# Decode attention over two key-value caches: the V loads move to ScalarE's DMA queue

## The chip, the cores and the metric

The kernel runs on one core of one Trainium2 chip. The metric is the device time of one execution in microseconds. The core has five engines with an instruction stream each (TensorE, or PE; VectorE, or DVE; ScalarE, or ACT; GpSimd, or POOL; SyncE, or SP) and 16 DMA engines that move data between HBM and the core's SBUF. A DMA is issued by an instruction in the stream of SP or ACT[...].

## The reference

Two problems, A and B, each one decode step of attention with 32 heads, a head size of 128 and one query. The caches have 16,384 keys. A attends to all of them, B to the last 4,096.

```python
q = (x @ wq).reshape(B, Sq, Hq, Dh)            # transposed to heads first
scores = jnp.einsum("bhqd,bhkd->bhqk", q, k) * (Dh ** -0.5)
p = _softmax(scores, axis=-1)
o = jnp.einsum("bhqk,bhkd->bhqd", p, v)
return o.reshape(B, Sq, Hq * Dh) @ wo          # transposed back first
```

In B, k and v are `cache[:, :, Sk - W:, :]` with W = 4096. All of it is bf16: K and V of A are 134 MB each, of B 34 MB each, wq and wo 4 MB for each problem. The two outputs of 512 numbers are joined.

## The kernel before

The caches are read in 20 loads, 16 for A and 4 for B, numbered i = 0 to 19; each has a K part and a V part of 8.39 MB. A load of A is two heads: a partition holds 256 keys of 128 numbers in one run of 64 KB, and 64 partitions hold a head. A load of B is two DMAs (U = 2, u = 0 and 1) of four heads each, with runs of 32 KB. Three buffers of 64 KB per partition take them: `kt` has two slots, K(i) going to slot (i+1) mod 2, and `vt` is one buffer for V. Before V(0), `vt` holds wq; after V(18) it takes wo. The last V, V(19), goes to the slot of `kt` that K(18) has left. `_alloc` lays this out.

Each engine runs a program written out by hand, and semaphores order them. The work on load i:

- VectorE multiplies K(i) by the query in place (`mult`, L304, 17.2 us in A; two instructions of 8.7 us in B), then adds the two halves of the head size in place (`add`, L315). Between the two it reduces the previous load's result to scores (`scores(i-1)`, L321), and after them it collects the previous load's output (`pick(i-1)`, L335 to L342). So its order is mult(i), scores(i-1), add(i), pick(i-1). Loads 0 and 1 are cut into four and two parts.
- TensorE sums the remaining 64 products in PSUM (`red(i)`, 32 matmuls), then multiplies the probabilities by V (`pv(i)`, 64 matmuls), then adds the picked result to `f`. Its order is red(i), pv(i), pick's matmul, red(i+1). After load 15 and after load 19 it normalises a problem (`norm`), and last come the products with wo, first of A, then of B in five pieces. Nearly all its matmuls are recorded under one helper's line, L379.
- ScalarE computes the exps of load i once scores(i) is there (L233): two for an A load, eight for a B load. It also copies the queries out of PSUM (L222), scales the output rows (`_orow`, L248) and issues the loads of x (L216).
- GpSimd only makes constants and passes on counts between VectorE and TensorE.
- SyncE issues all other DMAs, in `_sync_program`. It waits in order: K(i) goes out when red(i-2) has freed its slot (semaphore `s_red`); V(i-1) goes out next, when pv(i-2) has freed `vt` (`s_pv`). K(1) and V(0) wait for the end of the matmuls that read wq (`s_q`). V(19) goes out when red(18) is done. Then SP waits for pv(18) and issues the seven pieces of wo, and last the output.

All loads by SP go through one DMA queue, so the data of K(1), V(0), K(2), V(1) and so on arrive in this order.

In the lists above "pv(i)" means both halves u for a B load. The semaphores of V are `s_v[u]`, and `s_vlast[u]` for V(19); TensorE waits for them before the matmuls of pv.

Of the kernel before, what the change touches and what calls it, by code (L numbers as in the profile page):

```python
# [20 lines left out]
NB = 4  # L21
# [98 lines left out]
def _slot(i):  # L120
    return (i + 1) % 2


def _p_view(cx, st, u):
    return cx.p[u][:, 0 : st.keys * st.R].rearrange("p (t g e) -> p t g e", g=st.R, e=4)


def _sync_program(nc, cx, loads):
    e = nc.sync
    stA, stB = cx.sts  # L130
    for st in cx.sts:
        st.s_wq.on(e.dma_start(out=st.wq_t, in_=st.wq.rearrange("(p c) f -> p c f", c=st.KC)), 16)

    def kv(st, i, which):
        j = i if st is stA else i - stA.L
        view = st.k_view if which == "k" else st.v_view
        last = which == "v" and i == len(loads) - 1
        for u in range(st.U):
            h0 = (j * st.U + u) * st.R
            k0 = u * st.keys  # L140
            if which == "k":
                out = cx.kt[:, _slot(i), k0 : k0 + st.keys, :]
                sem = cx.s_k[_slot(i)][u]
            elif last:
                out = cx.kt[:, _slot(i - 1), k0 : k0 + st.keys, :]
                sem = cx.s_vlast[u]
            else:
                out = cx.vt[:, k0 : k0 + st.keys, :]
                sem = cx.s_v[u]
            ins = e.dma_start(out=out, in_=view[h0 : h0 + st.R].rearrange("g (i l) d -> i g l d", l=st.keys))  # L150
            sem.on(ins, 16)

    pv = 0
    kv(loads[0], 0, "k")
    for i in range(1, len(loads)):
        if i == 1:
            cx.s_q.wait(e, stA.N // stA.R // 512 + stB.N // stB.R // 512)
        else:
            cx.s_red.wait(e, NB * (i - 1))
        kv(loads[i], i, "k")  # L160
        if i > 1:
            pv += loads[i - 2].U
            cx.s_pv.wait(e, pv)
        kv(loads[i - 1], i - 1, "v")
    n = len(loads)
    cx.s_red.wait(e, NB * (n - 1))
    kv(loads[-1], n - 1, "v")
    cx.s_pv.wait(e, pv + loads[-2].U)
    for st, j0, m, sem in cx.pieces:
        src = st.wo.rearrange("(p j) f -> p j f", j=st.J)  # L170
        sem.on(e.dma_start(out=st.wo_t[:, j0 : j0 + m, :], in_=src[:, j0 : j0 + m, :]), 16)  # L171
    for st in cx.sts:
        st.s_row.wait(e, len(st.out_at))
        cx.s_end.on(e.dma_start(out=cx.out[0, 0:1, st.at : st.at + st.DN], in_=cx.row[0:1, st.at : st.at + st.DN]), 16)
    cx.s_end.wait(e, 32)
# [35 lines left out]
def _scalar_program(nc, cx, loads):  # L211
    e = nc.scalar
    stA, stB = cx.sts
    cx.s_pool.wait(e, 1)
    for w, st in enumerate(cx.sts):
        st.s_x.on(e.dma_start(out=cx.row[0:1, w * st.D : (w + 1) * st.D], in_=st.x[0, 0:1, :]), 16)  # L216
    n = 0
    for st in cx.sts:
        m = st.N // st.R // 512
        n += m  # L220
        cx.s_q.wait(e, n)
        st.s_qall.on(e.copy(st.qall[:, :], cx.red[:, 0:m, :].rearrange("p j f -> p (j f)")))  # L222
    cx.s_dve.wait(e, cx.n_off)
    for i, st in enumerate(loads):
        if i == stA.L:
            _orow(e, cx, stA)
        cx.s_sc.wait(e, i + 1)
        j = i if st is stA else i - stA.L
        for u in range(st.U):
            p = _p_view(cx, st, u)  # L230
            for g in range(st.R):
                h = st.f_at + (j * st.U + u) * st.R + g
                ins = e.activation(  # L233
                    out=p[:, :, g, :],
                    in_=cx.sc[:, u * st.keys : (u + 1) * st.keys].rearrange("p (t e) -> p t e", e=4),
                    func=ACT.Exp, scale=SCALE, bias=st.off[:, g : g + 1], accum_out=cx.cs[:, h : h + 1],
                )
            cx.s_p.on(ins)
    _orow(e, cx, stB)
    w = stB.DN // 2  # L240
    stB.s_o.wait(e, 1)
    stB.s_row.on(e.copy(cx.row[0:1, stB.at + w : stB.at + 2 * w], cx.out_ps(stB)[1]))


def _orow(e, cx, st):
    at = st.f_at
    st.s_recip.wait(e, 1)
    st.s_orow.on(e.activation(  # L248
        out=cx.orow[at : at + H, :], in_=cx.f[at : at + H, 0:DH], func=ACT.Copy, scale=cx.recip[at : at + H, 0:1],
    ))  # L250
# [233 lines left out]
def kernel(  # L484
# [49 lines left out]
    cx.out_ps = lambda st: [cx.red[r : r + 1, b, 0 : st.DN // len(st.out_at)] for r, b in st.out_at]  # L534

    _sync_program(nc, cx, loads)
    _pool_program(nc, cx)
    _vector_program(nc, cx, loads)
    _scalar_program(nc, cx, loads)
    _tensor_program(nc, cx, loads)  # L540

# [29 lines left out]
```

The softmax here doesn't subtract the row's maximum and nothing guards it: scores larger than these inputs give would overflow.

## Time and profile before

| what | value |
|---|---|
| time, median of 3 runs (range) | 822.37 us (822.32 to 822.43) |
| the profiled execution: time, and its span from first to last instruction | 822.22 us, 820.0 us |
| busy: PE, DVE, ACT, POOL | 341.2, 603.8, 35.5, 4.3 us |
| read from HBM | 352.32 MB, 430 GB/s over the span |
| mult of A, each (x, with the parts) | 13,810 ns mean of 20; a whole one 17.23 us |
| waits of DVE's mult for K of A | 150.7 us in 15 waits |
| waits of SP's K and V issues for pv, for red | 423.4 us in 18, 304.1 us in 20 |
| from issue to landing, median: K of A, V of A | 37.2 us, 31.3 us |

The profile gives one execution. Its rows name an engine, a line of the kernel, the operation, the output and the inputs by the program's names; "SPq" and "ACTq" are rows of an instruction queue that issues a DMA. A row of the timeline begins with its start and its length in us, and ends, in brackets, with the idle time of the engine before it and what ended that. A landing time counts from the issue, so it includes whatever stands ahead in the queue. The waits of SP are long because it has nothing else to do.

### The profile page before, as it was taken

Reading aid. Unit: us, or ns where it says so; the run is one execution under the profiler, and the core shown is the slowest. Engines: PE = TensorE matmul, PEld = TensorE weight load, DVE = VectorE, ACT = ScalarE, POOL = GpSimd, SP = SyncE. Lnnn points to the kernel's source line nnn. Section 1 sums busy time; section 2 is a strip of 40 time slices with the busy share of each in tenths; the row PEclk is TensorE's granted clock in tenths of the full one; section 3 lists DMA queues with packets and bytes.
Section 4 is the critical chain, followed back from the end, with each engine's and each line's share of the span. In section 5 each row is a group of like instructions: output and inputs, shape, how many; then the busy total and the mean of one; then the engine's idle time right before and its main releaser. Section 6 shows DMA issues by size and latency. Waiting matters only on the chain. (4 is left out here: it accounts for less than half of the span.)

```text
span 820.0 us, 5953 instructions
## 1 busy us (share of the span) xinstructions
PE 341.2 (42%) x2149; PEld 128.6 (16%) x2149; DVE 603.8 (74%) x167; ACT 35.5 (4%) x134; POOL 4.3 (1%) x14
## 2 busy tenths in 40 slices
PE   3433346152424244352608071534243353616276
PEld 1110112020101011110202020211011121202022
DVE  2089995959595968768595959595959969696921
ACT  0100000000000000000000000000000001010110
POOL 2000000000000000000000000000000000000000
PEclk9855668595856675656766575958566766756589
DMA  9999999999999999999999999999999999999997
GB/s 384 436 457 412 457 412 457 412 454 416 454 416 451 416 451 419 451 419 448 422 441 429 435 435 428 441 419 451 416 454 411 456 412 435 435 435 435 435 423 325
DMA packets 8222, 352.41 MB, mean 430 GB/s; under 512 B 916, under 2 KB 920, under 8 KB 1304
## 3 DMA queue, kind: packets, MB, share of 16 engines
q1 hardware_dynamic: 8212, 352.33, 99.4%
q8 instruction: 4, 0.07, 0.0%
q14 instruction: 2, 0.02, 0.0%
q10 hardware_dynamic: 4, 0.00, 0.0%
HBM read 352.32 MB, written 0.00 MB: 430 GB/s over the span
## 5 line engine op out<-in xcount | busy, mean ns | idle before, releaser
L304 DVE TENSOR_TENSOR kt<-kt,qallA 128x32768 bf16<-128x32768 bf16 (+2 forms) x20 | 276.2, 13810 | 150.7 <-DMA kt<-in_A_k_cache_dram 150.7
L379 PE MATMUL acc<-vt,p 128*8 128x512 bf16 (+1 forms) x1216 | 113.1, 550 | 348.3 <-PEq L42 348.3
L379 PE MATMUL red<-kt,ident 128*128 x640 | 183.2, 457 | 43.1 <-PEq L42 43.1
L315 DVE TENSOR_TENSOR kt<-kt 128x16384 bf16<-128x16384 bf16 (+2 forms) x24 | 174.5, 7269 | 0.8
L379 PEld LDWEIGHTS acc<-vt,p 128*8 128x8 bf16 (+1 forms) x1216 | 37.1, 114 | 423.5 <-issue 416.5
L379 PEld LDWEIGHTS red<-kt,ident 128*128 128x128 bf16 x640 | 72.5, 113 | 150.3 <-issue 103.6
L304 DVE TENSOR_TENSOR kt<-kt,qallB 128x16384 bf16<-128x16384 bf16 x8 | 69.5, 8691 | 13.4 <-DMA kt<-in_B_k_cache_dram 13.4
L321 DVE TENSOR_REDUCE sc<-red 128x256 f32<-128x2048 f32 x20 | 45.7, 2284 | 8.0 <-PE red L379 8.0
L233 ACT ACTIVATE p<-sc,offA 128x256 bf16<-128x256 f32 x32 | 16.0, 500 | 604.5 <-DVE sc L321 604.5
L379 PE MATMUL f<-s,win 128*32 128x128 f32 x48 | 11.2, 323 | 62.4 <-PEq L42 62.4
L379 PE MATMUL red<-vt,kt 128*128 128x512 bf16 x64 | 16.1, 416 | 4.6 <-DMA vt<-in_A_wq_dram 2.5
L233 ACT ACTIVATE p<-sc,offB 128x128 bf16<-128x128 f32 x32 | 12.4, 389 | 113.4 <-DVE sc L321 113.4
L342 DVE TENSOR_REDUCE s<-acc 128x128 f32<-128x512 f32 x24 | 16.6, 691 | 0.8
L379 PEld LDWEIGHTS f<-s,win 128*32 128x32 f32 x48 | 4.2, 121 | 72.9 <-issue 72.6
L337 DVE TENSOR_TENSOR acc<-acc,maskA 128x512 f32<-128x512 f32 x16 | 11.1, 692 | 0.0
L335 DVE COPY win<-selB 128x32 f32<-128x32 f32 x8 | 1.4, 178 | 11.3 <-PE acc L379 11.3
L379 PEld LDWEIGHTS red<-vt,kt 128*128 128x128 bf16 x64 | 6.6, 105 | 13.7 <-issue 7.8
L379 PE MATMUL red<-vt,ocA 128*1 128x512 bf16 x32 | 7.2, 379 | 0.0
L379 PE MATMUL acc<-kt,p 128*16 128x512 bf16 x64 | 5.3, 505 | 4.3 <-PEq L42 4.3
L335 DVE COPY win<-selA 128x32 f32<-128x32 f32 x16 | 2.8, 174 | 5.4 <-PE acc L379 5.4
L233 ACT ACTIVATION_READ_ACCUMULATOR p<-sc,offB 128x1 f32 x32 | 6.0, 187 | 0.0
L233 ACT ACTIVATION_READ_ACCUMULATOR p<-sc,offA 128x1 f32 x32 | 6.0, 187 | 0.0
(47 smaller groups left out, 36.8 us busy)
## 6 DMA issues: line engine op xcount, KB each, us to landing
kt<-in_B_k_cache_dram SPq DMA_DIRECT2D x8, 4096.0 KB, 34.8
vt<-in_B_v_cache_dram SPq DMA_DIRECT2D x6, 4096.0 KB, 29.0
kt<-in_B_v_cache_dram SPq DMA_DIRECT2D x2, 4096.0 KB, 36.6
vt<-in_A_wq_dram SPq DMA_DIRECT2D x1, 4096.0 KB, 12.2
vt<-in_B_wq_dram SPq DMA_DIRECT2D x1, 4096.0 KB, 21.4
vt<-in_A_wo_dram SPq DMA_DIRECT2D x2, 2048.0 KB, 23.1
vt<-in_B_wo_dram SPq DMA_DIRECT2D x1, 2048.0 KB, 29.7
vt<-in_B_wo_dram SPq DMA_DIRECT2D x1, 1024.0 KB, 31.6
```

The lines of the kernel that those rows point to most:

```text
L233: ins = e.activation(out=p[:, :, g, :], in_=cx.sc[:, u * st.keys : (u + 1) * st.keys].rearrange("p (t e) -> p t e", e=4), func=ACT.Exp, sc ...
L304: n = did(e.tensor_tensor(out=k, in0=k, in1=q.rearrange("p (o d) -> p o d", o=1).broadcast_to([P, b - a, DH]), op=ALU.mult,))
L315: cx.s_half.on(e.tensor_tensor(out=k[:, :, 0 : DH // 2], in0=k[:, :, 0 : DH // 2], in1=k[:, :, DH // 2 : DH], op=ALU.add,))
L321: cx.s_sc.on(e.tensor_reduce(out=cx.sc[:, :], in_=cx.red[:, :, :].rearrange("p b (k w) -> p (b k) w", w=W), axis=AX.X, op=ALU.add,))
L335: did(e.tensor_copy(cx.win[u][:, :], st.sel[:, at : at + H]))
L337: n = did(e.tensor_tensor(out=acc, in0=acc, in1=st.mask[:, :].rearrange("p (x o) -> p x o", o=1).broadcast_to([P, 4, DH]), op=ALU.mult,))
L342: cx.s_pick.on(e.tensor_reduce(out=cx.s[u][:, :], in_=acc.rearrange("p x d -> p d x"), axis=AX.X, op=ALU.add,))
L379: mm = lambda *a, **k: e.matmul(*a, skip_group_check=True, **k)
```

## The change

The function that issues a K or V part becomes `_kv`, which takes the issuing engine as an argument. SP keeps wq, all K parts, wo and the outputs. The V parts are issued in ScalarE's program, before the exps of the same load: V(0) after the copies of the queries, V(i) after a wait for pv(i-1), V(19) after a wait for red(18). The waits are the same as SP's were. ScalarE's issues go to its own DMA queue. Buffers, sizes and the programs of the other engines stay as they are.

```diff
-    pv = 0
-    kv(loads[0], 0, "k")
+    _kv(e, cx, loads, 0, "k")
     for i in range(1, len(loads)):
         if i == 1:
             cx.s_q.wait(e, stA.N // stA.R // 512 + stB.N // stB.R // 512)
         else:
             cx.s_red.wait(e, NB * (i - 1))
-        kv(loads[i], i, "k")
-        if i > 1:
-            pv += loads[i - 2].U
-            cx.s_pv.wait(e, pv)
-        kv(loads[i - 1], i - 1, "v")
-    n = len(loads)
-    cx.s_red.wait(e, NB * (n - 1))
-    kv(loads[-1], n - 1, "v")
-    cx.s_pv.wait(e, pv + loads[-2].U)
+        _kv(e, cx, loads, i, "k")
+    cx.s_pv.wait(e, sum(st.U for st in loads[:-1]))
     for st, j0, m, sem in cx.pieces:
...
     for i, st in enumerate(loads):
         if i == stA.L:
             _orow(e, cx, stA)
+        if i == len(loads) - 1:
+            cx.s_red.wait(e, NB * i)
+        elif i:
+            cx.s_pv.wait(e, sum(s.U for s in loads[:i]))
+        _kv(e, cx, loads, i, "v")
         cx.s_sc.wait(e, i + 1)
```

`_kv` has the body of the nested `kv`, with `e` as the issuing engine and the load's index in place of its problem:

```python
def _kv(e, cx, loads, i, which):
    st = loads[i]
...
    for u in range(st.U):
...
        ins = e.dma_start(out=out, in_=view[h0 : h0 + st.R].rearrange("g (i l) d -> i g l d", l=st.keys))
        sem.on(ins, 16)
```

More of the change, by code (lines that the diff above doesn't have):

```diff
@@ L125, in _p_view @@
     return cx.p[u][:, 0 : st.keys * st.R].rearrange("p (t g e) -> p t g e", g=st.R, e=4)
+def _kv(e, cx, loads, i, which):
+    st = loads[i]
+    stA = cx.sts[0]
+    j = i if st is stA else i - stA.L
+    view = st.k_view if which == "k" else st.v_view
+    last = which == "v" and i == len(loads) - 1
+    for u in range(st.U):
+        h0 = (j * st.U + u) * st.R
+        k0 = u * st.keys
+        if which == "k":
+            out = cx.kt[:, _slot(i), k0 : k0 + st.keys, :]
+            sem = cx.s_k[_slot(i)][u]
+        elif last:
+            out = cx.kt[:, _slot(i - 1), k0 : k0 + st.keys, :]
+            sem = cx.s_vlast[u]
+        else:
+            out = cx.vt[:, k0 : k0 + st.keys, :]
+            sem = cx.s_v[u]
+        ins = e.dma_start(out=out, in_=view[h0 : h0 + st.R].rearrange("g (i l) d -> i g l d", l=st.keys))
+        sem.on(ins, 16)
 def _sync_program(nc, cx, loads):
@@ L132, in _sync_program @@
         st.s_wq.on(e.dma_start(out=st.wq_t, in_=st.wq.rearrange("(p c) f -> p c f", c=st.KC)), 16)
[L134 to L151, printed above, removed]
-    pv = 0
-    kv(loads[0], 0, "k")
+    _kv(e, cx, loads, 0, "k")
     for i in range(1, len(loads)):
```

## The prediction

> **What bounds the kernel now.** I read the page first: its slices, its queue table and its chain.
>
> ```profile
> DMA  9999999999999999999999999999999999999997
> ...
> q1 hardware_dynamic: 8212, 352.33, 99.4%
> ...
> DMA vt<-in_B_wo_dram 4%; PE acc L379 0%; SPq L171 0%; DVE row L373 0%; PE red L379 0%
> ```
>
> The 16 DMA engines are full in every slice but the last, all on one queue (q1, SP's), and the chain ends in the wo load. Two stretches of the trace give the rate (columns: stretch, length, busy time of PE, PEld, DVE, ACT, POOL, clock, DMA share, GB/s):
>
> ```profile
> 330.00:640.00 310.00, 125.87 (x792) 46.70 (x790) 242.70 (x49) 8.74 (x32) 0.00 (x0) 0.67 1.00 433
> 640.00:780.00 140.00, 58.13 (x376) 21.73 (x378) 115.28 (x36) 11.02 (x53) 0.00 (x0) 0.67 1.00 434
> ```
>
> So 434 GB/s whatever the engines do. A load of K or V (128 rows x 65,536 B = 8.39 MB) takes 19.3 us, a K and V pair 38.6 us; 352.3 MB take 812 of the 820.0 us. No order of the same bytes saves more than the few us at the ends. What an order can do is leave DMA with nothing to do. For that I read when SP issues, and what VectorE does:
>
> ```profile
> 1.90 30.12 SPq L150 DMA_DIRECT2D kt<-in_A_k_cache_dram  x2
> 32.07 0.61 SPq L150 DMA_DIRECT2D vt<-in_A_v_cache_dram  x1
> 73.67 0.54 SPq L150 DMA_DIRECT2D kt<-in_A_k_cache_dram  x1
> 87.79 0.54 SPq L150 DMA_DIRECT2D vt<-in_A_v_cache_dram  x1
> 110.86 0.54 SPq L150 DMA_DIRECT2D kt<-in_A_k_cache_dram  x1
> ```
>
> ```profile
> 371.92 17.23 DVE L304 TENSOR_TENSOR kt<-kt,qallA 128x32768 bf16<-128x32768 bf16 x1 [9.10 <-DMA kt<-in_A_k_cache_dram]
> ...
> 410.51 17.23 DVE L304 TENSOR_TENSOR kt<-kt,qallA 128x32768 bf16<-128x32768 bf16 x1 [9.02 <-DMA kt<-in_A_k_cache_dram]
> ```
>
> K(9) lands at 371.9 (mult starts), K(10) at 410.5. After K(9), pv(8) ends and V(9) is issued at 398.13 (+26.2); red(9) ends and K(11) is issued at 411.63 (+39.7). In one queue the order is K(10), V(9), K(11): at 398.13 K(10) still needs 12.4 us, at 411.63 V(9) needs 18. That is the cover; VectorE idles 9 us per cycle. It is the late issue of a load, not work, that could hurt.
>
> [...] the trace shows 434, so I expect no gain in rate. The trace shows the turns once, at the start:
>
> ```profile
> 1.92 0.51 ACTq L216 DMA_DIRECT2D row<-in_A_x_dram  x1
> ...
> 8.01 0.29 PE L379 MATMUL oc_ps<-one,row 1*128 1x1 bf16 x4 [2.45 <-DMA row<-in_A_x_dram]
> ```
>
> A 1 KB load on ACT's queue, issued at 1.92 behind 8.4 MB of wq and 8.4 MB of K(0), is there at 8.01, when even the first wq (13.2, by its 12.2 us to landing) is not. So ACT's queue goes between SP's, though some packets late: 6.1 us for 1 KB is what some four wq packets of 1.2 us take (32 KB each; estimate from 434 GB/s over 16 engines). K and V packets of problem A are equal (64 KB), so the shares are half and half.
>
> **The change part by part.**
>
> *Removed from SP, added on ACT.* Twenty-four V issues (0.54 us per A load, 1.18 per B pair, from SP's rows) move to ScalarE, which is busy 35.5 of 820 us. They run before the wait for scores: nothing. V(i)'s wait for pv(i-1) adds nothing for the exps behind it: scores(i) comes after pick(i-1) on VectorE, which waits for pv(i-1) anyway. V(16) now stands behind orow of A: 667.5 becomes 670.3, 2.8 us, under other loads: nothing, at most 3. K no longer stands behind V's waits on SP, but K's wait (red) is met before V's (pv), so K's issue rule is unchanged.
>
> *Moved in time: the sharing.* V no longer stands behind the K issued before it but takes half the engines. No bytes more; but K lands later, and what K's landing releases is issued later.
>
> *Start.* V(0) is issued at 32.6, once ScalarE's copies end (31.50 + 1.01). K(0) (lands 43.7), K(1) and V(0) are 50 us of data from 31.5, done at about 81 in any order. In one queue K(1) was there by 63, before VectorE could take it (70.3). In turns K(1) lands last, at 82: mult(1) is 11.7 us late, so V(1)'s issue goes from 87.8 to 99.5 and K(3)'s from 110.9 to 122.5. DMA then has K(2) alone (issued at 73.7): 81 to 100.3; V(1), about 1 us after its issue, 100.6 to 119.9; K(3) at 123.6. Nothing moves for 0.3 + 3.7 us. If V(0) cuts into K(0) too, K(0) lands at 50 and V(0) at 74, K(1) still at 82; red(0) and so K(2) come 7 us later, still within 81. I take 4.5 us; bounds 3 and 6.
>
> *Middle.* I stepped the loads forward with offsets from before: K(i) lands, exps(i-1) end 20.6 later; pv(i-1), 5.9, starts when they and V(i-1) are there and issues V(i); red(i) ends 40 after K(i)'s landing and issues K(i+2); first data 1 after an issue; half rate while both queues have work. One pair of cycles: K(5) lands at 222, exps(4) end at 242.6, V(4) lands at 243.5, pv(4) issues V(5) at 249.4. K(6) has been alone from 243 and lands at 263; red(5) issues K(7) at 262, which shares with V(5). V(5) lands at 289.5, pv(5) issues V(6) at 295.4, and K(7) lands at 299; then the pattern repeats. K's intervals alternate between 41 and 36, mean 38.6. The tightest point is the last: K(7)'s data end at about 298, V(6)'s begin at 296.4, so some 2 us of cover are left of 12. As long as it holds the middle costs nothing.
>
> *End.* V(19) took the slot of K(18) and was issued at 755.61 by SP. On ACT it stands behind the exps of load 18:
>
> ```profile
> 755.61 1.18 SPq L150 DMA_DIRECT2D kt<-in_B_v_cache_dram  x2
> 781.37 0.81 SPq L171 DMA_DIRECT2D vt<-in_A_wo_dram  x2
> ```
>
> Those end at 772.7 in the trace, 17 us after 755.61. The same stepping brings V(17) at 756, by its sharing and the start's 4.5 us, so pv(17) ends at 759 (before 743); then pick 1.5, mult(19) 17.3 (before it waited for K(19) until 748.9), scores 2.3, exps 3.3: V(19) is issued at about 784. K(19) and V(18) are done at 782.5 (before 778, plus 4.5); V(19)'s data start at 785 to 786: 3.5 us dry (bounds 0 and 5). wo is issued after pv(18), at 789; with wo rows of 16 KB and V rows of 32 KB, V(19) has two thirds of the engines from some 790 on: 4.3 us of its 19.3 are done, the other 15 take 22, so it lands near 812. wo ends when both are through, 786 + 38.6 + 1 = 826.
>
> PE then becomes the end. Before:
>
> ```profile
> 803.46 7.24 PE L379 MATMUL red<-vt,ocA 128*1 128x512 bf16 x32
> 812.01 1.91 PE L379 MATMUL red<-vt,ocB 128*1 128x256 bf16 x32 [1.31 <-DMA vt<-in_B_wo_dram]
> ...
> 816.90 0.38 PE L379 MATMUL red<-vt,ocB 128*1 128x256 bf16 x4 [0.21 <-DMA vt<-in_B_wo_dram]
> ```
>
> PE's products with wo come after pv(19) in program order, 7.24 + 1.91 + 1.04 + 1.03 + 0.38 = 11.6 us, and waited for wo. Now: V(19) at 812, last half of pv 2.7, picks and norm 3.0 (800.5 to 803.5 before): 817.7; products to 829.3; copy and store 2.7 (817.3 to 820.0 before): 832. By wo alone it would be 826 + 0.4 + 2.7 = 829.
>
> *Sum.* Dry 4.5 + 3.5, products past the last wo 3: 11; the chain of the end by itself gives 832 - 820 = 12. I take 11.5, a span of 831.5. The profiled execution took 822.22 with its span of 820.0; 822.22 + 11.5 = 833.7. The runs' median is 822.37, 0.15 more, below the rounding of the steps.
>
> **Rivals.**
>
> *Not slower.* The engines take whole transfers in order of issue. Then K(1) precedes V(0) as now, nothing is dry, and V(19), 17 us later, still comes before V(18) ends at 778 and before wo: 822.4. It decides if K(1) lands before 70.3. Against it: the 1 KB load above.
>
> *The middle dries out.* The margin of 2 us is gone, because shares are unequal or an issue takes longer to start. One us lost per cycle on some 15 cycles gives 833.7 + 15 = 849. At the extreme, V always first, the same steps lose 9.7 us on every second cycle: 895. For it: the margin is thin. Against: equal packets.
>
> *The rate falls.* Two streams of 64 KB rows on one engine cost 1%: 812 x 0.01 = 8 us more, 842. Nothing in the trace shows it; the rate was 433 and 434 in the two stretches, with rows of 64 and 32 KB.
>
> *Faster.* Only a rate over 434[...]. Then the losses above must be absent as well.
>
> **How the numbers follow.** Forecast 0.70 (its own range 828 to 838), not slower 0.09, middle dry 0.11, rate 0.08, faster 0.02. About 0.2% (1.6 us) is what a measurement of this kernel can tell from no change. Slower by more: 0.70 + 0.11 + 0.08 = 0.89; within: 0.09; faster: 0.02. The range 827 to 843 takes in the forecast with the bounds of its costs (dry 3 to 11, products 0 to 3) and the rate case; it leaves out the not-slower case and the dried-out middle.
>
> **What would show it.** ACT's queue with some 168 MB (20 loads of 8.39); mult(1) at about 82 with a wait for K; K(3) issued near 122; intervals of K that alternate but average 38.6; 434 GB/s in the middle; V(19) issued near 784; the chain ending in PE's wo products, not in DMA. Wrong: K(1) landing at 63, a middle average over 39, or a rate off 434.

## The result and the profile after

The changed kernel took 843.48 us at the median of four runs (840.08 to 847.53), beside 822.35 for the kernel before: a ratio of 1.0259, interval 1.0212 to 1.0306, slower. A second series of five runs gave 842.27 (840.37 to 845.07), ratio 1.0245 (1.0225 to 1.0264). So the loss is some 20 us where 11.5 were forecast, and its direction is the forecast's. The runs of the changed kernel lie up to 7 us apart; those of the kernel before lie within 0.2 us. The profiled execution is the slowest of the first four (847.53, span 845.3), so what is read from it is somewhat more than the median loses.

On its page the queue table now has two rows, and the chain (by engine) no longer begins with DMA:

```profile
q1 hardware_dynamic: 4756, 184.55, 50.8%
q10 hardware_dynamic: 3460, 167.78, 46.7%
...
PE 2%; DVE 0%; ACT 0%; issue 0%
```

q10 is ScalarE's queue, with the 167.8 MB of V. The two shares add to 97.5% of the span, 99.4% before. Where the rest went is read from two stretches, the start and the loads 2 to 15. Before, then after (columns as above: the last two are DMA share and GB/s):

```profile
14.00:130.00 116.00, 48.92 (x257) 17.90 (x255) 84.69 (x21) 5.06 (x10) 0.00 (x0) 0.69 1.00 434
130.00:640.00 510.00, 205.71 (x1293) 76.64 (x1294) 391.26 (x81) 14.21 (x52) 0.00 (x0) 0.67 1.00 434
```

```profile
14.00:130.00 116.00, 44.95 (x194) 16.43 (x192) 73.76 (x18) 3.97 (x6) 0.00 (x0) 0.64 0.95 407
130.00:640.00 510.00, 186.30 (x1274) 70.14 (x1274) 385.92 (x79) 14.20 (x52) 0.00 (x0) 0.70 1.00 427
```

At 434 GB/s the first stretch would have needed 116 x 407 / 434 = 108.8 us: 7.2 are lost at the start. The second loses 510 x (1 - 427 / 434) = 8.2, where the prediction had nothing. The remaining 10 us are after 640. Note that the DMA share still reads 1.00 in the second stretch: the rows that DMA moves took longer there, which is taken up below.

VectorE's waits show what became late (longest in total, times, longest one):

```profile
DVE win L335 <- PE acc L379: 113.2, 18, 11.8
DVE kt L304 <- DMA kt<-in_A_k_cache_dram: 87.4, 14, 39.0
```

Before, VectorE waited 150.7 us for K of A and 16.8 us for pv (the row `win` is the first instruction of pick). Now the larger wait is for pv, which waits for V. The half-and-half share is seen when queue shares are taken from a stretch in which K and V are both under way, 53 to 68 us (columns: rows, which the page calls packets and which are 64 KB here, MB, and their time as a share of the 16 engines'):

```profile
q10 hardware_dynamic: 51, 3.34, 51.4%
q1 hardware_dynamic: 49, 3.21, 49.4%
```

The start went as follows:

```profile
51.46 4.43 DVE L304 TENSOR_TENSOR kt<-kt,qallA 128x8192 bf16<-128x8192 bf16 x1 [39.04 <-DMA kt<-in_A_k_cache_dram]
...
82.73 8.69 DVE L304 TENSOR_TENSOR kt<-kt,qallA 128x16384 bf16<-128x16384 bf16 x1 [4.54 <-DMA kt<-in_A_k_cache_dram]
```

K(0) is taken at 51.5 (43.7 before), K(1) at 82.7 (70.3 before). And the end: the last two V issues and, from the chain in order of time, PE's products with wo.

```profile
791.10 0.54 ACTq L146 DMA_DIRECT2D kt<-in_B_v_cache_dram  x1
...
791.67 0.62 ACTq L146 DMA_DIRECT2D kt<-in_B_v_cache_dram  x1
```

```profile
830.30 12.33 PE red L379 x92
```

V(19) is issued at 791.1; the last products begin when pv(19) is through, and take 12.3 us to the end's copy and store.

### The profile page after: what moved, and what is told of

Read it like the earlier page. It is cut to its first block, busy times and chain, and to the rows that moved or that the text cites. A ratio compares the mean times of both kernels' runs of the same rounds, so it can differ in the third digit from the quotient of the medians.

```text
span 845.3 us, 5952 instructions
## 1 busy us (share of the span) xinstructions
PE 328.6 (39%) x2149; PEld 124.6 (15%) x2149; DVE 604.3 (71%) x167; ACT 35.5 (4%) x134; POOL 4.3 (1%) x14
## 5 line engine op out<-in xcount | busy, mean ns | idle before, releaser
L379 PE MATMUL acc<-vt,p 128*8 128x512 bf16 (+1 forms) x1216 | 110.7, 541 | 389.1 <-PEq L42 389.1
L379 PE MATMUL red<-kt,ident 128*128 x640 | 171.2, 427 | 51.1 <-PEq L42 51.1
L379 PEld LDWEIGHTS red<-kt,ident 128*128 128x128 bf16 x640 | 68.2, 107 | 149.8 <-issue 101.1
L233 ACT ACTIVATE p<-sc,offB 128x128 bf16<-128x128 f32 x32 | 12.4, 388 | 113.1 <-DVE sc L321 113.1
L379 PE MATMUL acc<-kt,p 128*16 128x512 bf16 x64 | 7.2, 627 | 9.0 <-PEq L42 9.0
L379 PE MATMUL red<-vt,ocA 128*1 128x512 bf16 x32 | 9.7, 479 | 0.0
```

What stands on the lines that cost most here:

```text
L233: ins = e.activation(out=p[:, :, g, :], in_=cx.sc[:, u * st.keys : (u + 1) * st.keys].rearrange("p (t e) -> p t e", e=4), func=ACT.Exp, sc ...
L379: mm = lambda *a, **k: e.matmul(*a, skip_group_check=True, **k)
```

## The experiments

Each run stands beside runs of the kernel before on the same chip.

| run | what it does | us, median | over before | ratio (interval) |
|---|---|---|---|---|
| v0_sp | V(0) back on SP's queue | 840.59 | 18.3 | 1.0232 (1.0212 to 1.0252) |
| vlast_sp | V(19) back on SP's queue | 847.41 | 25.1 | 1.0304 (1.0282 to 1.0325) |
| both_sp | V(0) and V(19) back | 843.36 | 21.1 | 1.0255 (1.0231 to 1.0279) |
| both_sp_pvhalf | the same, pv of A halved | 836.03 | 13.8 | 1.0172 (1.0153 to 1.0191) |
| before_vlate | one queue, V(19) issued late | 822.19 | 0.0 | 1.0000 (0.9991 to 1.0008) |
| before_pv2 | one queue, pv of A twice | 822.14 | -0.1 | 1.0000 (0.9992 to 1.0009) |
| after_pv2 | changed kernel, pv of A twice | 861.04 | 38.8 | 1.0474 (1.0458 to 1.0490) |
| mid_only | only V(1) to V(15) on ACT's queue | 833.90 | 11.7 | 1.0153 (1.0134 to 1.0171) |
| mid_only_pvhalf | the same, pv of A halved | 829.12 | 6.9 | 1.0087 (1.0073 to 1.0101) |
| mid_only_k32 | mid_only, K rows of 32 KB | 861.99 | 39.8 | 1.0484 (1.0466 to 1.0502) |
| mid_only_v32 | mid_only, V rows of 32 KB | 894.96 | 72.7 | 1.0886 (1.0871 to 1.0901) |
| after_again | the changed kernel again | 842.27 | 20.0 | 1.0245 (1.0225 to 1.0264) |
| end_sp | V(16) to V(19) back on SP's queue | 836.99 | 14.7 | 1.0182 (1.0165 to 1.0199) |
| v8_only | only V(8) on ACT's queue | 824.06 | 1.8 | 1.0023 (1.0012 to 1.0034) |

### Single loads put back

In `_sync_program`, after the K issue, and with the load taken out of ScalarE's loop:

```diff
         _kv(e, cx, loads, i, "k")
+        if i == 1:
+            _kv(e, cx, loads, 0, "v")
+    cx.s_red.wait(e, NB * (len(loads) - 1))
+    _kv(e, cx, loads, len(loads) - 1, "v")
     cx.s_pv.wait(e, sum(st.U for st in loads[:-1]))
```

(v0_sp has the first two new lines, vlast_sp the last two, both_sp all four.)

> V(0) alone goes back to SP's queue, behind K(1); the other V loads stay on ACT's. Theory 'empty queues' (what the change costs is time in which neither queue has work, because sharing delays what releases the next issues: about 6.6 us at the start, about 8 in the middle, the rest from V(19) on): K(0) lands at 43 and K(1) before 70 again, the dry stretch at 80 to 84 and at 123 goes, and the time falls by about 6, to 837 (835 to 839). Rival 'slower packets' (two queues make the engines themselves slower, whatever the order): 842 to 844.

> V(19) alone goes back to SP's queue, ahead of wo, issued when red(18) is done. 'Empty queues': V(19) no longer waits for the exps of load 18 and no longer shares with wo, so PE's products with wo again wait for wo and not for V(19): 8 us less, 836 (834 to 839). 'Slower packets': within 2 us of the changed kernel, 842.

> V(0) and V(19) both on SP's queue; only V(1) to V(18) are on ACT's. 'Empty queues': the middle's share stays, where V(i) lands late, pv follows at once and V(i+1) is issued when K's data have just ended: 8 us over the kernel before, 830 (827 to 832), and less even from run to run than the kernel before. The prediction's own step (the middle costs nothing): 823. 'Slower packets': 838 or more.

v0_sp missed both ranges: 840.6. The stretch from 14 to 130 us is back at 434 GB/s, but the time falls by 2 to 3 us, not by 6. A little of the gain is lost again later: from 130 to 640 us this run has 426 GB/s, where the changed kernel's profile has 427, which is 1.2 us of the 510.

vlast_sp missed, in the other direction: 847.4. SP's queue is now busy with V(19) while ACT's queue has V(18), and V(18) lands later; that it has half the engines, as V(0) had from 53 to 68 us (51 and 49 rows), is an estimate: its share was not read here. PE's pv(18) shows the delay (the row is its second half):

```profile
805.88 3.53 PE L380 MATMUL acc<-vt,p 128*16 128x512 bf16 x32 [9.97 <-PEq L42]
```

In the changed kernel both halves were done at 797.0; here V(18)'s second half is taken only at 805.9. All that follows pv(18) is a chain of its own: in the kernel before, pv(18) ends at 781.3 and the program at 820.0. It was covered by wo's data there; now V(18)'s lateness goes straight into it. both_sp missed as well: 843.4, where 830 was expected and 823 by the prediction's step. That is a number which 'slower packets' had allowed (838 or more); the time of a row, below, speaks against it.

### What costs in one queue

```diff
     cx.s_red.wait(e, NB * (n - 1))
+    cx.s_sc.wait(e, n - 1)
     kv(loads[-1], n - 1, "v")
```

> The kernel before, with one wait more: SP issues V(19) only when scores(18) are there, some 14 us later than before, about as late as ScalarE's order makes it, but still in the one queue. 'Sharing' (late issues cost nothing while the queue holds V(18), and only the sharing of the engines between two queues costs): 822.3, within 0.5. 'Late issue' (the order of ScalarE's program costs by itself): 826 to 830.

822.2, with V(19) issued at 769.6 instead of 755.6. A V(19) that is 14 us late costs nothing by itself: in one queue V(18) still lies ahead of it (in the kernel before PE takes V(18)'s second half at 778.1). So the wait for the exps, which ScalarE's order puts before V(19), is not the loss at the end as long as there is one queue.

The second pair doubles pv:

```diff
-            for t in range(T):
+            for t in [*range(T)] * (2 if st is stA else 1):
```

> The kernel before, with the product with V of problem A made twice over (128 matmuls instead of 64, the second pass starting anew, so the output is the same): pv takes some 11.5 us instead of 5.7. One queue: V(i) is issued when K(i+1) still has 12.4 us to go, K when V has 18, so 6 us more are covered: 822.3 to 823. If pv were on the path in one queue too: 16 x 5.7 = 91 us more.

> The changed kernel, with the product with V of problem A made twice over as in the run beside it. 'pv in the loop' (with two queues V(i) lands late, pv follows at once, and V(i+1) can be issued only then, so that every us of pv is a us without work for DMA): 4 to 5 us more per load of A, 880 to 920. The prediction's cover of 2 us plus what the sharing gives back: 850 to 865. pv not in the loop: 842 to 848.

With the longer pv the kernel before keeps 822.1, the changed one goes from 842 to 861. pv took 8.8 us instead of about 5.7 (not 11.5 as expected), so 3.1 us more per load cost 19 us over 16 loads, 1.2 us each. 861 lies in the range given for the prediction's cover, but that range was worked out for 5.8 us more per load. What is shown is that pv stands in the loop, and that not every us of it is lost. The stretch from 130 to 640 us, before_pv2 and then after_pv2:

```profile
130.00:640.00 510.00, 229.13 (x2149) 89.79 (x2141) 391.42 (x82) 14.22 (x52) 0.00 (x0) 0.76 1.00 434
```

```profile
130.00:640.00 510.00, 213.36 (x2082) 83.69 (x2082) 368.63 (x78) 14.21 (x52) 0.00 (x0) 0.75 0.96 408
```

The first has more PE work in the same time than the second and a full DMA; the second has 408 GB/s.

### The middle by itself

mid_only issues V(1) to V(15) from ScalarE and all other V from SP, in the order of the kernel before:

```diff
         _kv(e, cx, loads, i, "k")
+        if i == 1 or i > stA.L:
+            if i > 1:
+                cx.s_pv.wait(e, sum(st.U for st in loads[: i - 1]))
+            _kv(e, cx, loads, i - 1, "v")
+    cx.s_red.wait(e, NB * (len(loads) - 1))
+    _kv(e, cx, loads, len(loads) - 1, "v")
```

> Only V(1) to V(15) on ACT's queue; V(0) and V(16) to V(19) back in SP's, in the order of the kernel before. Start and end are then as before, with the last data some 3 us ahead of the end: 822.4 plus the middle's loss, which the account of the profiles puts at 7 to 8: 829 to 832. If the middle costs nothing by itself, 823. If the loss simply moves (as in the runs with V(0) or V(19) alone on SP's queue), 838 or more.

833.9, somewhat above the 829 to 832 expected, and the end is again that of the kernel before, a chain through wo's DMA. Its middle has this row:

```profile
130.00:640.00 510.00, 181.55 (x1294) 68.77 (x1298) 389.12 (x80) 15.29 (x56) 0.00 (x0) 0.70 0.99 424
```

510 x (1 - 424 / 434) = 11.8 us, against 11.7 measured in the time: the whole loss of this kernel is time in which its DMA engines moved less than 434 GB/s.

Halving pv:

```diff
-            T = st.keys // 4
+            T = st.keys // 4 if st is stB else st.keys // 8
```

> As both_sp, but the first product with V of problem A leaves out the second half of the keys of every partition (32 of 64 matmuls), so pv takes about 3 us instead of 6 and V(i+1) is issued some 3 us earlier after V(i) landed. No byte less is loaded. 'Empty queues': if pv stands in the loop that leaves DMA without work, most of the middle's loss goes: 823 to 825. 'Slower packets': as both_sp.

> As mid_only, and the product with V of problem A leaves out the second half of the keys of every partition (32 of 64 matmuls): pv takes some 3 us instead of 6, all loads stay. 'V's loop' (DMA runs out of work in the middle because V(i+1) is issued only after pv, which now follows V's late landing): 3 us of cover come back, 823 to 827 after mid_only's 833.9. If the middle's loss has to do with the engines and not with pv: 832 to 835.

Half the matmuls made pv 3.6 us long, 2 us shorter than before. This brings back 7.3 us of both_sp's loss and 4.8 of mid_only's 11.7, less than expected in both (836.0 and 829.1). So pv's part in the middle is real, and 'slower packets' alone, which gave no gain, is excluded. Whether the remaining 6.9 us (429 GB/s in the same stretch) come from the 3.6 us of pv that are left or from something else is not settled. PE's granted clock was lower as well, 0.667 in this profile against 0.717 in mid_only's; what that did to PE's other work was not measured.

### Other shares

K rows, or V rows, of problem A at half the size, in `_kv`; the waits for that load go from 16 to 32:

```diff
-        ins = e.dma_start(out=out, in_=view[h0 : h0 + st.R].rearrange("g (i l) d -> i g l d", l=st.keys))
-        sem.on(ins, 16)
+        src = view[h0 : h0 + st.R].rearrange("g (i l) d -> i g l d", l=st.keys)
+        n = st.keys // 2 if which == "k" and st is stA else st.keys
+        for a in range(0, st.keys, n):
+            sem.on(e.dma_start(out=out[:, a : a + n, :], in_=src[:, :, a : a + n, :]), 16)
```

> As mid_only, but each K load of problem A goes out as two DMAs with rows of 32 KB, V's rows stay at 64 KB. If the engines take turns row by row, V gets two thirds of the bytes while both queues have work: V's data last 23 us instead of 27 to 28, K's some 31 instead of 27. 'V's loop': V lands earlier, the cover before V(i+1)'s issue grows by 4 to 5 us and the middle is full again: 823 to 827. If K's late landing counts as much as V's: 834 or more. If turns go by bytes: no change, 834.

> As mid_only, but each V load of problem A goes out as two DMAs with rows of 32 KB, K's rows stay at 64 KB. Row by row, V gets one third while both queues have work: V's data last some 32 us. 'V's loop': V lands 4 to 5 us later, 2 to 3.5 us lost per load, 850 to 880. If K's late landing counted as much as V's: no worse than 834. If turns go by bytes: 834.

The shares are as expected, row by row. In mid_only_v32, from 332 to 354 us (98 rows each, but V's are half as long):

```profile
q1 hardware_dynamic: 98, 6.42, 67.3%
q10 hardware_dynamic: 98, 3.15, 33.1%
```

In mid_only_k32, from 346 to 372 us, V has 8.06 MB and K 3.15. But the times missed: V with one third costs 72.7 us, more than the 28 to 58 expected, and V with two thirds does not cure the middle. It costs 39.8 us. VectorE's waits tell the two apart, mid_only_v32 first:

```profile
DVE win L341 <- PE acc L385: 211.7, 19, 15.0
```

```profile
DVE kt L310 <- DMA kt<-in_A_k_cache_dram: 188.8, 8, 32.0
```

In the first, VectorE waits for pv, that is for V. In the second it waits for K: the longest of the 8 waits is K(0)'s at the start, the other seven are 21 to 24 us long. With 28.1% of the engines' time for K's queue (346 to 372 us; 71.5% for V's), every second K is late, mult after it, and so scores, exps, pv and the next V's issue (V issues are 30 and 52 us apart in turn). V's loop alone was too narrow a theory: in these two runs the load with about a third of the engines became the late one, and the half-and-half share of the changed kernel is the mildest of the three tried (11.7 us in mid_only).

### The terms of the sum

end_sp is mid_only with V(0) left on ACT's queue. v8_only has V(8) alone there:

```diff
         _kv(e, cx, loads, i, "k")
+        if i != 9:
+            if i > 1:
+                cx.s_pv.wait(e, sum(st.U for st in loads[: i - 1]))
+            _kv(e, cx, loads, i - 1, "v")
```

> The changed kernel once more, unchanged, timed in the same rounds as the two runs beside it, since its times spread over 7 us: 840 to 848 on each run, median 842 to 845. It is the base for the size of the start and of the end.

> V(0) to V(15) on ACT's queue, V(16) to V(19) back in SP's in the order of the kernel before. If the end's part is the 7 us by which the run with only V(0) on SP stood above mid_only (840.6 against 833.9), this gives 836 to 838, and the start's part is what is left over mid_only: 2 to 4. If the start costs the 6.7 us by which the profiles differ in their first 130 us: 839 to 842.

> Only V(8) on ACT's queue, all else in SP's as before. 'Loss per load' (each shared load leaves DMA without work for some 0.7 us, 11 us over 15 loads): 823. 'Entry' (what costs is the change from whole transfers to shared ones, in which K and V fall out of step once): 825 to 829. No sharing by one load can cost nothing at all: 822.2 if the queue's cover of 12 us holds.

end_sp came where the first case put it. The steps from run to run give the terms, each good to some 2 us by the intervals: before to mid_only 11.7, mid_only to end_sp 3.1 (V(0)), end_sp to the changed kernel 842.27 - 836.99 = 5.3 (V(16) to V(19)); together 20. The terms hold for this order of steps: taking V(0) back from the changed kernel itself gave 2 to 3 us, and taking V(19) back made it slower.

v8_only costs 1.8 us, between the two cases expected, clear of nothing (1.0012 to 1.0034) and above the 0.7 of an even loss per load. Fifteen such loads would cost 27, so loads in a row cost less than single ones. How the middle's 11.7 us divide into entry and repetition is not settled by these runs.

## Why the prediction was wrong

**Right: the bound, the direction, the sharing.** DMA was the bound at 434 GB/s, and the engines served both queues at once. Before the result there was one 1 KB load to show it (issued at 1.92, there at 8.01), which gives no shares; half and half was the author's estimate. Measured, both queues get about equal numbers of rows (51 and 49 above), and in the runs with rows of 32 KB the shares are about 1 to 2 (33.1% to 67.3% in mid_only_v32, 28.1% to 71.5% in mid_only_k32).

A falling rate was put up as a rival, with an assumed loss of 1%, and its number, 842, is about what was measured. Its cause is not: while both queues are at work, a row takes 0.514 x 16 x 15 / 51 = 2.42 us (from the rows for 53 to 68 us above). Four stretches of the changed kernel show where the middle lost:

```profile
258.00:304.00 46.00, 17.89 (x126) 6.64 (x119) 31.15 (x10) 1.09 (x4) 0.00 (x0) 0.69 0.99 410
304.00:378.00 74.00, 24.85 (x166) 9.48 (x168) 57.63 (x9) 2.18 (x8) 0.00 (x0) 0.68 1.00 435
378.00:384.00 6.00, 3.49 (x40) 1.43 (x33) 4.04 (x4) 0.00 (x0) 0.00 (x0) 0.98 0.64 229
384.00:532.00 148.00, 51.05 (x345) 19.16 (x347) 114.31 (x21) 4.38 (x16) 0.00 (x0) 0.70 1.00 432
```

V(5) and V(6) are issued in the first (259.7 and 300.6), V(8) in the third (379.9), each when the rows of the K ahead are through or all but through. V(7) is issued in the second (336.0), with K's rows still to come, and nothing is lost. The queue rows for 380 to 384 us, first of the changed kernel, then of the kernel before:

```profile
q10 hardware_dynamic: 16, 1.05, 76.6%
```

```profile
q1 hardware_dynamic: 19, 1.25, 71.8%
```

So the first 16 rows of V(8) took 0.766 x 16 x 4 / 16 = 3.06 us each, while 0.718 x 16 x 4 / 19 = 2.42 us is usual. Counted row by row from 130 to 640 us, the engines were without a row for 3.6 us, and rows longer than 2.42 us took 5.5 us more; all but 0.4 us of both lies within 8 us after the issue of a V. So next to nothing is lost while both queues have rows (435 GB/s from 304 to 378 us); the sharing costs by making V late, so that the next V is issued when little or nothing is left ahead of it. Why the first rows are then longer is not shown.

**Start: 4.5 forecast; 3.1 in the time, 7.2 in the stretch itself.** K(1) at 82.7 (forecast 82), V(1) issued at 100.4 (99.5), K(3) at 123.5 (122.5). V(0) did cut into K(0), the variant the prediction named and then dismissed with "K(2) come 7 us later, still within 81": K(2) was issued at 82.39, after the data had run out:

```profile
80.00:84.00 4.00, 2.35 (x6) 0.61 (x4) 1.26 (x1) 0.00 (x0) 0.00 (x0) 0.50 0.69 229
```

More was lost there than forecast, but part of it comes back later: end_sp moved 413 GB/s in the first stretch, mid_only 434, but 427 against 424 in the second. That the 3.1 lies near the forecast is in part luck.

**Middle: nothing forecast, 11.7 measured. This is the step that failed**, in the words of the prediction: "some 2 us of cover are left of 12. As long as it holds the middle costs nothing". The 2 us came from a strictly alternating pattern with fixed durations, and they were taken to be enough. The real pattern is not regular. Three V issues in a row of the changed kernel:

```profile
300.64 0.54 ACTq L146 DMA_DIRECT2D vt<-in_A_v_cache_dram  x1
...
336.02 0.54 ACTq L146 DMA_DIRECT2D vt<-in_A_v_cache_dram  x1
...
379.92 0.54 ACTq L146 DMA_DIRECT2D vt<-in_A_v_cache_dram  x1
```

Intervals of 35.4 and 43.9 us, where the steps gave 36 and 41. pv itself varies (5.1 us at 330.8, 6.3 at 294.3), and with V landing late each variation moves the next issue; that this alone makes the pattern irregular is not shown. Nor were 2 us of cover free: V(3), V(4) and V(11) (181.2, 219.5, 496.1), whose first rows began 2.1 to 2.7 us after the issue, behind the last of K's, lost 0.2 to 0.4 us each by the count above. From V(3) at 181.24 to V(15) at 649.72 the mean is 468.48 / 12 = 39.0 us, not 38.6. That, and a rate off 434, are two of the signs of being wrong that the prediction had named. It had priced the loss of this cover at 1 us per cycle, as a rival with a chance of 0.11. What came is 11.7 / 15 = 0.8 per load in mid_only, or 8.2 us in the changed kernel's own profile: that rival, a little smaller.

**End: 3.5 dry plus 3 of products forecast; 5.3 measured.** V(19)'s issue (791.1, forecast 784, the difference being about the middle's) and the chain in PE's products are as described; the products took 12.3 us (11.6). The parts are not. Changed kernel first, kernel before last:

```profile
790.00:797.00 7.00, 4.86 (x64) 1.84 (x64) 6.96 (x2) 3.19 (x16) 0.00 (x0) 0.66 0.96 342
833.00:845.30 12.30, 9.61 (x90) 4.75 (x88) 1.10 (x2) 0.37 (x1) 0.00 (x0) 0.89 0.08 31
```

```profile
815.00:820.00 5.00, 1.77 (x24) 0.53 (x18) 0.42 (x1) 0.37 (x1) 0.00 (x0) 0.95 0.09 35
```

Before V(19)'s data 7 x (1 - 342 / 434) = 1.5 us were lost. After the last data the changed kernel runs on for some 11 us and the kernel before for some 5, so that the products cost nearly 7 us more, not 3. That the sum comes near the forecast is luck. The two thirds of the engines for V(19) beside wo were an estimate too; the queue rows for 800 to 808 us (13 of q10's are under 512 B) give V(19) 2.10 of 3.36 MB, 0.62:

```profile
q10 hardware_dynamic: 77, 2.10, 61.0%
q1 hardware_dynamic: 77, 1.26, 36.8%
```

What the prediction did not see is that pv(18) has a chain of the same length behind it; vlast_sp showed it.

**Not slower, faster:** excluded by the intervals. 842 to 843 is at the upper edge of the range of 827 to 843, and just outside it in the first series; the range went that far only for the rate rival, whose cause did not come.

**Sums.** Two do not close, and neither touches the forecast. The lower bounds (dry 3, products 0) give 825.4, which is under the range's 827. And 895 for V always first is 822.4 + 7.5 x 9.7, while the case beside it counts from 833.7.

## What to carry to other kernels

In the kernel before, which is bound by DMA, the one queue is also a schedule: the loads land one after the other, in the order of their issue and of their need. V(8), K(10), V(9) and K(11) are there at 391.2, 410.5, 429.8 and 449.1 us (issue plus time to landing), 19.3 apart. In the changed kernel a second queue split the engines (51 and 49 rows from 53 to 68 us) between the load that is needed now and the one that is needed next; K(0) and K(1) were taken 7.8 and 12.4 us later, VectorE's waits for pv grew from 16.8 to 113.2 us, and every issue that waits for a consumer of one of them came later. Before splitting a queue, count the cover of every issue, that is how much data lies ahead of it when it is made, and take a cover of the size of the variation of the work in the loop as no cover. A DMA share of 1.00 does not show that nothing is lost (427 GB/s from 130 to 640 us, against 434 before, both at 1.00); compare the GB/s.

None of the versions tried beats the kernel before, and none that moves the same bytes at 434 GB/s can by much: its last data come at about 817 of 820 us.

## What had not been expected of the hardware

- The same bytes in two queues lose their evenness: 7 us between runs of the changed kernel (840.1 to 847.5), 0.9 at most between 25 of the kernel before (821.9 to 822.8). PE's granted clock varies in the kernel before as well (0.56 to 0.67 of full speed in four pv stretches), whose time keeps within those 0.9 us. Whether the clock is the cause of the spread, once pv stands in the loop, was not tried.
- The two queues' shares went by row and not by byte, so that the size of a row was a weight: with 32 KB against 64 KB (mid_only_v32, 98 rows each) the engines gave 33 to 67, and a change that leaves bytes and order alone moved the time from 833.9 to 895.0 us.
- The first rows of V(8), before which the rows of the other queue had just run out, cost more: 3.06 us on average for the first 16, against 2.42.
